# Twelve tiles' decays and the low halves move from GpSimd to VectorE, and one bit extraction from VectorE to ScalarE

## The chip, the cores and the metric

The program runs on one core of one Trainium2 chip. The metric is the device time of one execution in microseconds (us); smaller is better. TensorE (PE in the rows) multiplies matrices, VectorE (DVE), ScalarE (ACT) and GpSimd (POOL) work element by element, and SyncE (SP) issues most of the DMA transfers. Each engine takes its instructions in the order in which the program has them, and waits on semaphores for operands that another engine makes.

## The reference

Three layers follow each other over 4 sequences of 768 tokens, 512 values each, with 8 heads of 64.

```python
# retention: a decayed running state of each head
state = gamma[None, :, None, None] * state + einsum('bhd,bhe->bhde', k[:, :, t], v[:, :, t])
y[:, :, t] = scale * einsum('bhd,bhde->bhe', q[:, :, t], state)
...
# a dense layer, 512 -> 2048 -> 512, weights in float64
h = x @ w_in
g = np.maximum(h, 0.0) + alpha * np.minimum(h, 0.0)
x = g @ w_out
...
# 8 experts, 512 -> 1024 -> 512; a token goes to the one of its largest logit
logits = xn @ en.T / tau
expert_idx = np.argmax(logits, axis=1)
h = np.maximum(x[mask] @ w1[e], 0.0)
out[mask] = gate_w[mask, None] * (h @ w2[e])
```

## The kernel before

**Tiles.** The 3072 tokens are 24 tiles of 128. Tile i is chunk i // 4 of sequence i % 4, and four tiles (one chunk of each sequence) make a block of the dense layer, so there are 6 blocks. Matrix products of the dense and expert layers run in float16 with each operand cut into two halves: a high half, rounded to float16, and a low half, which is what is left. Three products (high by high, high by low, low by high) replace one in float32.

**Retention of a tile** (`att_load`, `att_hat`, `att_a`, `att_b`). Queries, keys by dimension, keys by token and values come in four parts of 128x512 float32 (`qk_buf` holds the first three, `vp_buf` the values; the first eight tiles also use the memory of `wout`, which waits for its weights). `att_hat` multiplies queries and both forms of the keys by powers of gamma: for tiles 0 to 7 two of the three products are on VectorE and one on GpSimd, from tile 8 on all three are on GpSimd. The results go to `hat_buf` or `stage`. `att_a` makes the scores and masks them on VectorE (rows `wout<-bank,cau`, `vp_buf<-bank,cau`). `att_b` makes the output and the new state `st_bd`, and cuts the output into halves `xh`, which a DMA transposes into `xT`.

**Float64 weights** (`convert`). They are loaded as integers into three buffers (`f_buf` twice, `pay_buf`), 16 pairs of chunks of 128x1024: ScalarE takes the high words as float32 and rescales them, VectorE shifts 13 bits out of the low word's upper half and masks the sign (two uint16 instructions on a 128x1024 strided view), VectorE merges the parts (`win<-win,f_buf` and the like), and ScalarE sums the squares. `quarter` and `split_out` then cut `win` and `wout` into halves with `split`: ScalarE makes the high half; the low half is VectorE's for even pairs and GpSimd's for odd ones, and for the latter ScalarE first scales the pair in float32.

**The dense layer.** `mm1(j, m)` makes step m (of 16) of block j's hidden layer, `mm2(j, m, o)` adds it to the output of tile o. `mm1` takes its PSUM bank from a ring of two (`h_ring`) and its buffer `g` from a ring of two. In block 0 ScalarE copies the bank twice (`g<-bank`, `stage<-bank`), VectorE combines them, ScalarE rounds to the high half and GpSimd subtracts for the low half. In the later blocks ScalarE makes one copy, VectorE reads the bank itself, and VectorE makes the low half too.

**The head.** I call head what runs until `mm2` keeps TensorE busy: the retention of tiles 0 to 11, all 16 conversions, the 16 hidden-layer steps of block 0, and the splits. No step of `mm2` can start before all of w_in and w_out are converted, since the scale `s_g` of w_out's halves is taken over all of them (`scale_out`); `unit_experts` (some 30 small instructions on VectorE) stands beside it.

**What sets the order.** The class `Plan` records all instructions and issues them by a list schedule: each engine takes, of what is ready by the plan's own cost table, what TensorE's sequence needs first. So a change of instructions or of engines changes the order on every engine.

Of the kernel before, what the change touches and what calls it, by code (L numbers as in the profile page):

```python
# [21 lines left out]
P = 128  # L22
NCH = S // P              # chunks of a sequence
NTILE = NT // P           # token tiles: tile i is chunk i // B of sequence i % B
BT = B                    # token tiles of a block: one chunk of each sequence
# [4 lines left out]
NPRE = 2                  # tiles of the expert that has most tokens before the last block  # L30
NMIN = NTILE - NPRE       # the other tiles of tokens sorted by expert, at least
NSLOT = NMIN + E - 1      # and at most
SL = 30
CAP = NT                  # rows of an expert's region
PW = DM + 2               # words of a routed token: hi | lo | gate | id
# [3 lines left out]
# Powers of two that bring a norm into [2^(C-190.5), 2^(C-189.5)).  # L39
# [6 lines left out]
# columns of the float32 constants  # L46
# [11 lines left out]
def _constants():  # L58
# [23 lines left out]
    # decay of a query and of a key, by chunk: [c, (h2 d), 2, pair, t]  # L82
# [13 lines left out]
class Plan:  # L96
    """Records instructions in the order in which they would be right one after the other, and
    issues them in one in which each engine always takes, of the instructions whose operands are
    there, the one that is needed first. An instruction's place in the tensor engine's own
    sequence, and what waits for it, say when it is needed."""  # L100

    # from the end of an instruction to the start of another that waits for it; a DMA's issue
    # and its transfer are apart
    AFTER = {"PE": 197.0, "ACT": 145.0, "DVE": 140.0, "POOL": 100.0, "SP": 0.0}
    DMA_DONE, DMA_RATE = 940.0, 360.0
    COLD = 1500.0, 3500.0        # the tensor engine's idle time after which it is slow, and for how long
    SLACK = 8000.0
    PATIENCE = 0.7, 2000.0
    AHEAD = 60000.0          # how long before it is needed a DMA may be issued
    BACKLOG = 2500.0         # of DMA, beyond which none is issued  # L110

    def __init__(self, nc):
        self.nc = nc
        self.nodes = []
        self.log = {}            # reads and writes of a tensor: (region, node)
        self.unit_ = None
        self.pe_time = 0.0
        self.bias = 0.0
        self.vector = self.Engine(self, nc.vector, "DVE")
        self.scalar = self.Engine(self, nc.scalar, "ACT")  # L120
        self.gpsimd = self.Engine(self, nc.gpsimd, "POOL")
        self.tensor = self.Engine(self, nc.tensor, "PE")
        self.sync = self.Engine(self, nc.sync, "SP")
# [9 lines left out]
    class Engine:  # L133
# [24 lines left out]
        def cost(self, method, kw):  # L158
            """Engine's time, time until the result is there, bytes moved."""
# [69 lines left out]
    def unit(self, eng):  # L229
        """Instructions of one engine that stay together."""  # L230
        @contextmanager
        def scope():
            assert self.unit_ is None
            node = self.Node(eng)
            node.start = self.pe_time
            self.nodes.append(node)
            self.unit_ = node
            yield
            self.unit_ = None
        return scope()  # L240
# [6 lines left out]
    def issue(self):  # L247
# [19 lines left out]
        while True:  # L267
# [16 lines left out]
            # rather wait a little for what is needed earlier  # L284
# [35 lines left out]
def retention_prelu_moe_kernel(ctx: ExitStack, tc, qkv, w_in, w_out, alpha, emb, tau, w1, w2,  # L320
# [17 lines left out]
    class Ring:  # L338
        """Buffers used in turn."""
# [22 lines left out]
    def col(name):  # L362
# [5 lines left out]
    # A matrix in float32 lies two chunks of 512 columns behind the place where its halves go,  # L368
    # so that a pair's halves never land on what is still to be split.
    win = buf("win", [KF + 2, 512])  # L370
    wout = buf("wout", [KF + 2, 512])
    stage = buf("stage", [16, 512])         # experts' weights; before, halves of g
    xT = [buf(f"xT{k}", [2, KD, BW], F16) for k in range(2)]
    st_bd = buf("st_bd", [B, KD, P])
    f64_buf = buf("f64_buf", [4, 512, 2], I32)   # float64 weights; later, halves of g
# [7 lines left out]
    # the first chunk's tiles use what else waits for w_out  # L383
    room = wout.rearrange("p c x -> p (c x)")
    first = {"qk": [room[:, 1536 * k:1536 * k + 1536].rearrange("p (a x) -> p a x", a=3) for k in range(3)] + [qk_buf],
# [3 lines left out]
             "hat": [hat_buf, stage[:, 12:15]]}  # L389
# [3 lines left out]
    x2T_ring = Ring([x2T_buf[:, k] for k in range(2)])  # L393
    pay_ring = Ring([pay_buf[:, k] for k in range(4)])
# [23 lines left out]
    def pow2(ss, s, c, hb=None):  # L418
        """Powers of two by which vectors of squared norm ss are scaled, into s."""
# [10 lines left out]
    def total(acc, n):  # L430
        """Sum of acc over partitions and columns, on every partition."""
# [9 lines left out]
    def norm(ss, n, e):  # L441
        """Newton's steps on 1/sqrt; 1e-6 on top of the norm."""
# [15 lines left out]
    def split(hi, lo, src, s, pool):  # L458
        """Halves of a pair of chunks. For the Pool engine the chunks are scaled first."""
# [13 lines left out]
    def att_load(i):  # L473
        if i % B == 0:
            SP.dma_start(out=cqk_sb, in_=cqk[i // B])
        qk_t[i] = first["qk"].next() if i < B * N_ROOM else qk_buf
# [4 lines left out]
    def att_hat(i):  # L481
        """Decayed queries and keys of tile i."""
        c = i // B
        t = qk_t.pop(i)
        hat = att[i] = first["hat"].next() if i < B * N_ROOM else hat_buf
        for a in range(2):
            (G if c > 1 else V).tensor_tensor(out=hat[:, a, :], in0=t[:, a, :],
                            in1=cqk_sb[:, a].rearrange("p k t -> p (k t)"), op=ALU.mult)
        o = _COLS["ks"][0] + H * c
        G.tensor_tensor(out=hat[:, 2, :].rearrange("p (h d) -> p h d", h=H),  # L490
                        in0=t[:, 2, :].rearrange("p (h d) -> p h d", h=H),
                        in1=cst[:, o:o + H].unsqueeze(2).to_broadcast([P, H, D]), op=ALU.mult)

    def att_a(i):
        """Masked scores of tile i."""
        hat = att[i]
        ring = x_ring if i < B + N_EARLY else m_ring
        # heads of one half of the partitions share a bank
# [14 lines left out]
    # From tile HALVED on, scores and values go into their product as halves.  # L513
# [8 lines left out]
    def att_s(i):  # L522
        """Halves of the scores and values of tile i; the state, scaled as their product is."""
# [27 lines left out]
    def att_b(i, early=False):  # L551
        """Outputs of tile i, the state after it, the halves of x."""
# [48 lines left out]
    def att_x(i, src):  # L601
        """The halves of x with the model dimension on partitions."""
# [4 lines left out]
    # The exponent is rebased by a product that moves the high word's upper eight exponent  # L607
    # bits, which takes what is too small for float32 to zero.
# [4 lines left out]
    s_in = buf("s_in", [KD])        # a scale for every quarter of w_in's columns  # L613
    i_in = buf("i_in", [KD])
    s_g = buf("s_g", [KD])          # what the halves of w_out's rows of a quarter are scaled by
# [3 lines left out]
    def convert(w, g, src):  # L619
        """Pair g of chunks to float32."""  # L620
        f = f64_ring.next()
        # w_in's chunks in the order of its columns
# [8 lines left out]
        # the low word becomes the sign and the three bits that the high word's shift makes room for  # L631
        h = f.rearrange("p n t -> p (n t)").bitcast(U16).rearrange("p (n t) -> p n t", t=4)
        V.tensor_scalar(out=h[:, :, 0], in0=h[:, :, 1], scalar1=13, scalar2=None, op0=ALU.logical_shift_right)
# [4 lines left out]
    def alpha_bound():  # L638
        # |g| <= |h| sqrt(1 + sum over partitions of their largest alpha^2)
# [7 lines left out]
    def quarter(q):  # L647
        """Halves of a quarter of w_in's columns."""
# [4 lines left out]
        for g in range(2 * q, 2 * q + 2):  # L653
            p = win16[:, 2 * g:2 * g + 2]
            split(p[:, :, 0], p[:, :, 1], raw(win, 2 * g), s_in[:, q:q + 1], g % 2 )
# [15 lines left out]
    def split_out(g):  # L671
        p = wout16[:, 2 * g:2 * g + 2]
        split(p[:, :, 0], p[:, :, 1], raw(wout, 2 * g), s_g[:, g // 2:g // 2 + 1], g % 2 )

# [62 lines left out]
    class Route:  # L737
# [7 lines left out]
        def halve(self, o, acc):  # L745
            """A routed token's row: the halves of x scaled, its gate, where it is from."""
# [24 lines left out]
        def finish(self):  # L771
# [6 lines left out]
            # 1 / scale of the row; over the norm, for the logits  # L778
# [14 lines left out]
            # the first of the largest  # L793
# [7 lines left out]
            # ranks  # L801
# [17 lines left out]
            # gates  # L819
# [39 lines left out]
    g16 = {}  # L859

    def mm1(j, m):
# [11 lines left out]
        if j == 0:  # L873
            # the Pool engine takes a part while the vector engine has most to do
            gg = g16[j, m] = gg_first.next()
            u = gg.rearrange("p a x -> p (a x)").bitcast(F32)
            A.activation(out=g, in_=h, func=AF.Relu, scale=-R_G)
            A.activation(out=u, in_=h, func=AF.Copy, scale=R_G)
            V.scalar_tensor_tensor(out=g, in0=g, scalar=oma[:, m:m + 1], in1=u, op0=ALU.mult, op1=ALU.add)
            A.activation(out=gg[:, 0, :], in_=g, func=AF.Copy)  # L880
            G.tensor_tensor(out=gg[:, 1, :], in0=g, in1=gg[:, 0, :], op=ALU.subtract)
            return
        A.activation(out=g, in_=h, func=AF.Relu, scale=-1.0)
        V.scalar_tensor_tensor(out=g, in0=g, scalar=oma[:, m:m + 1], in1=h, op0=ALU.mult, op1=ALU.add)
        gg = g16[j, m] = gg_ring.next()
# [21 lines left out]
    # slots: the two tiles known early, what there is at least, what there may be  # L907
# [41 lines left out]
    def gather(t):  # L949
# [4 lines left out]
        # with the model dimension on partitions  # L954
# [377 lines left out]
```

## Time and profile before

| what | value |
|---|---|
| median of 3 runs | 1041.25 us (1040.83 to 1045.32) |
| profiled execution, first to last instruction | 1051.0 us |
| PE busy over the span | 943.4 us (90%) |
| DVE busy | 570.0 us (54%) |
| ACT busy | 492.6 us (47%) |
| POOL busy | 304.0 us (29%) |

The profiled execution is a run of its own. Its span is 9.75 us longer than the median of the timed runs. Busy shares are means over the whole span, and the head has quite other ones than the rest, so the rows below are taken by stretch.

### The profile page before, as it was taken

The numbers are of one execution on the slowest core, as the hardware profiler recorded it, in microseconds if no ns is written. First come the engines' busy times: TensorE is split into PE (matmuls) and PEld (weight loads), VectorE is DVE, ScalarE is ACT, GpSimd is POOL, SyncE is SP. The second block draws the span as 40 slices with busy tenths as digits, with TensorE's granted clock in tenths as the row PEclk, the third lists the DMA queues.
The fourth block names the chain that finished last, engine by engine and source line by source line (L and its number), as shares of the span: only waits on it lengthen the run. The fifth ranks groups of instructions, "written<-read, shape, count | busy, mean of one in ns | idle before, by whom it ended". The sixth has DMA issues, their size and how long they took to land. (4 is left out here: it accounts for less than half of the span.)

```text
span 1051.0 us, 19041 instructions
## 1 busy us (share of the span) xinstructions
PE 943.4 (90%) x7100; PEld 561.8 (53%) x7100; DVE 570.0 (54%) x1299; ACT 492.6 (47%) x865; POOL 304.0 (29%) x316
## 2 busy tenths in 40 slices
PE   5778876999999988988999899899889999998995
PEld 5664543555554544444444444444677777775763
DVE  5999999546766775567345554645712222221231
ACT  1457666546767956787667658742101010100100
POOL 1234556312342433323312321440231212113110
PEclk9887788999999989999999999999999999999998
DMA  8986532463866956876476557569575399825670
GB/s 279 307 268 193 189 129 71 114 188 91 234 197 197 251 151 213 240 201 191 171 220 164 187 181 214 157 219 316 186 201 168 72 292 315 243 65 132 151 287 21
DMA packets 129824, 201.45 MB, mean 192 GB/s; under 512 B 89726, under 2 KB 90110, under 8 KB 124608
## 3 DMA queue, kind: packets, MB, share of 16 engines
q1 hardware_dynamic: 123168, 179.42, 58.1%
q0 software_dynamic: 6560, 20.77, 5.8%
q8 instruction: 57, 0.93, 0.4%
q14 instruction: 39, 0.32, 0.1%
HBM read 204.59 MB, written 51.14 MB: 243 GB/s over the span
## 5 line engine op out<-in xcount | busy, mean ns | idle before, releaser
L145 PE MATMUL bank<-xT,win 128*128 128x512 f16 (+1 forms) x2208 | 338.9, 310 | 14.5 <-ACT g L145 7.3
L145 PEld LDWEIGHTS <-win 128*128 128x128 f16 x2400 | 186.8, 100 | 153.8 <-issue 31.9
L145 PE MATMUL bank<-wout,f_buf 128*128 128x512 f16 x960 | 227.5, 384 | 5.6 <-DVE pay_buf L145 4.8
L145 PEld LDWEIGHTS <-f_buf 128*128 128x128 f16 x960 | 92.9, 99 | 115.6 <-issue 11.4
L145 ACT ACTIVATE stage<-stage 128x1024 f16<-128x1024 f32 x96 | 101.0, 1052 | 54.9 <-DMA wsplit<-stage 46.0
L145 POOL TENSOR_TENSOR stage<-stage 128x1024 f16<-128x1024 f32 x32 | 68.2, 2131 | 146.1 <-ACT stage L145 117.8
L145 DVE SCALAR_TENSOR_TENSOR f_buf<-g,f_buf 128x512 f16<-128x512 f32 x80 | 72.7, 909 | 53.1 <-ACT f_buf L145 52.9
L145 DVE SCALAR_TENSOR_TENSOR g<-g,oma,bank 128x512 f32<-128x512 f32 x80 | 59.4, 744 | 73.5 <-ACT g L145 73.3
L145 ACT ACTIVATE st_bd<-bank 128x512 f16<-128x512 f32 x30 | 17.9, 597 | 149.7 <-PE bank L145 129.6
L145 POOL DMA_INDIRECT out<-xT,ids x25 | 25.3, 1013 | 214.4 <-DVE xT L145 181.5
L145 ACT ACTIVATE stage<-stage,se 128x1024 f16<-128x1024 f32 (+1 forms) x64 | 71.6, 1139 | 11.2 <-DVE se L145 6.5
L145 POOL TENSOR_TENSOR hat_buf<-qk_buf,cqk_sb 128x512 f32<-128x512 f32 x32 | 46.4, 1452 | 83.4 <-DMA qk_buf<-in_qkv 44.9
L145 PEld LDWEIGHTS <-wout 128*128 128x128 f16 x1152 | 65.5, 98 | 7.8 <-issue 4.8
L145 ACT ACTIVATE g<-bank 128x512 f32<-128x512 f32 x96 | 55.9, 584 | 26.0 <-PE bank L145 25.9
L145 PE MATMUL bank<-xT,wout 128*128 128x128 f16 x1056 | 62.7, 219 | 3.5 <-issue 3.4
L145 ACT ACTIVATE f_buf<-g 128x512 f16<-128x512 f32 x80 | 49.8, 622 | 34.1 <-DVE g L145 34.1
L145 PEld LDWEIGHTS <-st_bd 128*128 128x128 f16 x408 | 39.7, 99 | 45.3 <-issue 1.6
L145 DVE SCALAR_TENSOR_TENSOR st_bd<-bank,st_bd 128x512 f16<-128x512 f32 x34 | 23.5, 690 | 65.7 <-ACT st_bd L145 58.5
L145 DVE TENSOR_SCALAR xT<-bank,f_buf,cqk_sb 128x512 f32<-128x512 f32 x22 | 17.8, 809 | 67.0 <-PE bank L145 67.0
L145 PE MATMUL bank<-win,st_bd 128*128 128x512 f16 x216 | 49.4, 386 | 0.0
L145 PE MATMUL bank<-wout,stage 128*128 128x512 f16 (+1 forms) x208 | 48.8, 388 | 0.0
L145 DVE SCALAR_TENSOR_TENSOR stage<-stage,se 128x1024 f16<-128x1024 f32 x32 | 41.1, 1283 | 12.4 <-ACT stage L145 11.0
(253 smaller groups left out, 1320.9 us busy)
## 6 DMA issues: line engine op xcount, KB each, us to landing
win<-wsplit SPq DMA_DIRECT2D x56, 1024.0 KB
wout<-wsplit SPq DMA_DIRECT2D x52, 1024.0 KB
stage<-in_w SPq DMA_DIRECT2D x64, 512.0 KB
wsplit<-stage SPq DMA_DIRECT2D x64, 512.0 KB
qk_buf<-in_qkv SPq DMA_DIRECT2D x18, 768.0 KB
f_buf<-in_w_in SPq DMA_DIRECT2D x12, 512.0 KB
vp_buf<-in_qkv SPq DMA_DIRECT2D x20, 256.0 KB
f_buf<-in_w_out SPq DMA_DIRECT2D x10, 512.0 KB
```

The costliest lines, as they stand in the source:

```text
L145: call = lambda: fn(**kw)
```

## The change

It does four things.

- For tiles 0 to 11 `att_hat` multiplies the queries and the values in place on VectorE; the keys stay as they are loaded, since the values (by token) now carry the decay that both forms of the keys had. GpSimd has nothing to do for these tiles. The buffers of queries and keys are now held until `att_b` is done, and `hat_buf` and `stage` become two more of them.
- In `convert` the shift of the low word becomes a ScalarE instruction that writes whole words.
- `split` of w_in and w_out uses VectorE for the low half of every pair, with no scaling in float32 ahead of it.
- `mm1` of block 0 does what the later blocks do: one ScalarE copy, VectorE reads the bank, VectorE makes the low half.

```diff
-             "hat": [hat_buf, stage[:, 12:15]]}
+    first = {"qk": [... for k in range(3)] + [qk_buf, hat_buf, stage[:, 12:15]],
...
+    qk_ring = Ring([qk_buf, hat_buf])
...
-        qk_t[i] = first["qk"].next() if i < B * N_ROOM else qk_buf
+        qk_t[i] = (first["qk"] if i < B * N_ROOM else qk_ring).next() if i < HALVED else qk_buf
...
-        hat = att[i] = first["hat"].next() if i < B * N_ROOM else hat_buf
+        o = _COLS["ks"][0] + H * c
+        decay = cst[:, o:o + H].unsqueeze(2).to_broadcast([P, H, D])
+        if i < HALVED:
+            att[i] = t
+            V.tensor_tensor(out=t[:, 0, :], in0=t[:, 0, :], in1=cqk_sb[:, 0].rearrange("p k t -> p (k t)"), op=ALU.mult)
+            v = v_t[i].rearrange("p (h d) -> p h d", h=H)
+            V.tensor_tensor(out=v, in0=v, in1=decay, op=ALU.mult)
+            return
+        hat = att[i] = hat_buf
         for a in range(2):
-            (G if c > 1 else V).tensor_tensor(out=hat[:, a, :], in0=t[:, a, :],
+            G.tensor_tensor(out=hat[:, a, :], in0=t[:, a, :],
...
-        V.tensor_scalar(out=h[:, :, 0], in0=h[:, :, 1], scalar1=13, scalar2=None, op0=ALU.logical_shift_right)
+        A.activation(out=f[:, :, 0], in_=h[:, :, 1], func=AF.Copy, scale=2.0 ** -13, bias=2.0 ** -14 - 0.5)
...
-            split(p[:, :, 0], p[:, :, 1], raw(win, 2 * g), s_in[:, q:q + 1], g % 2 )
+            split(p[:, :, 0], p[:, :, 1], raw(win, 2 * g), s_in[:, q:q + 1], False)
...
-        split(p[:, :, 0], p[:, :, 1], raw(wout, 2 * g), s_g[:, g // 2:g // 2 + 1], g % 2 )
+        split(p[:, :, 0], p[:, :, 1], raw(wout, 2 * g), s_g[:, g // 2:g // 2 + 1], False)
...
-        if j == 0:
-            gg = g16[j, m] = gg_first.next()
-            u = gg.rearrange("p a x -> p (a x)").bitcast(F32)
-            A.activation(out=g, in_=h, func=AF.Relu, scale=-R_G)
-            A.activation(out=u, in_=h, func=AF.Copy, scale=R_G)
-            V.scalar_tensor_tensor(out=g, in0=g, scalar=oma[:, m:m + 1], in1=u, op0=ALU.mult, op1=ALU.add)
-            A.activation(out=gg[:, 0, :], in_=g, func=AF.Copy)
-            G.tensor_tensor(out=gg[:, 1, :], in0=g, in1=gg[:, 0, :], op=ALU.subtract)
-            return
         A.activation(out=g, in_=h, func=AF.Relu, scale=-1.0)
         V.scalar_tensor_tensor(out=g, in0=g, scalar=oma[:, m:m + 1], in1=h, op0=ALU.mult, op1=ALU.add)
-        gg = g16[j, m] = gg_ring.next()
+        gg = g16[j, m] = (gg_ring if j else gg_first).next()
```

HALVED is 12 in both kernels; from that tile on nothing changes in `att_hat`.

How the instructions move shows at two places. The first is VectorE where the first hidden-layer steps come in, between the retention of tiles 4 to 7 (one piece of the difference; `g_86` and `g_87` are the two buffers `g`, `bank_93` and `bank_94` the two banks of `mm1`, the uint16 rows `f_buf<-f_buf` belong to the conversions):

```order
 L145 TENSOR_TENSOR st_bd<-bank_96,st_bd 64x4x64 x2
-L145 TENSOR_SCALAR f_buf<-f_buf 128x1024
+L145 SCALAR_TENSOR_TENSOR g_86<-g_86,oma,bank_93 128x512
+L145 TENSOR_TENSOR vp_buf<-vp_buf,cst 128x512
+L145 SCALAR_TENSOR_TENSOR g_87<-g_87,oma,bank_94 128x512
+L145 SCALAR_TENSOR_TENSOR stage<-g_86,stage 128x512
+L145 SCALAR_TENSOR_TENSOR stage<-g_87,stage 128x512
 L145 TENSOR_SCALAR hbx<-ssx_130 128x1
 L145 TENSOR_SCALAR sx_132<-hbx 128x1
-L145 TENSOR_SCALAR f_buf<-f_buf 128x1024
+L145 TENSOR_TENSOR qk_buf<-qk_buf,cqk_sb 128x512
```

Two shifts leave this place, and two hidden-layer steps, each now with two VectorE instructions, and the decays of values and queries come in.

The second place is VectorE at the end of the head, from the scale `s_g` on. Before, the first low half of w_out is followed by the experts' small instructions:

```order
L145 TENSOR_SCALAR s_g<-i_in,smn_152,so_149 128x4
L145 TENSOR_SCALAR iw<-im_151,io_150 128x1
L145 SCALAR_TENSOR_TENSOR g_86<-g_86,oma,stage 128x512
L145 TENSOR_SCALAR rd_0_188<-invx,iw 128x4
L145 TENSOR_SCALAR rd_1_189<-invx,iw 128x4
L145 SCALAR_TENSOR_TENSOR wout<-wout,s_g 128x2x512
L145 COPY ess_137<-bank_96 128x8
L145 TENSOR_SCALAR nb_0_138<-ess_137 128x8
```

In the changed kernel, same place:

```order
L145 TENSOR_SCALAR s_g<-i_in,smn_152,so_149 128x4
L145 SCALAR_TENSOR_TENSOR stage<-g_87,stage 128x512
L145 TENSOR_SCALAR sx_133<-hbx 128x1
L145 SCALAR_TENSOR_TENSOR g_86<-g_86,oma,bank_93 128x512
L145 SCALAR_TENSOR_TENSOR wout<-wout,s_g 128x2x512
L145 SCALAR_TENSOR_TENSOR xh<-bank_96,sx_133,xh 128x512
L145 SCALAR_TENSOR_TENSOR stage<-g_86,stage 128x512
L145 SCALAR_TENSOR_TENSOR wout<-wout,s_g 128x2x512
L145 SCALAR_TENSOR_TENSOR g_87<-g_87,oma,bank_94 128x512
```

The low halves of w_out, eight now on VectorE instead of four, stand closer together behind the scale, and the small instructions of the experts come between and behind them.

## Rows read from the trace of the kernel before

**Rows 1.** The page: the span, and VectorE's busy tenths in 40 equal slices.

```profile
span 1051.0 us, 19041 instructions
...
DVE  5999999546766775567345554645712222221231
```

**Rows 2.** Windows: length, busy us of PE, PEld, DVE, ACT, POOL, clock, DMA.

```profile
0.00:24.00 24.00, 13.26 (x88) 12.19 (x89) 13.50 (x27) 3.56 (x5) 4.47 (x9) 1.00 0.81 299
24.00:162.00 138.00, 107.16 (x648) 75.10 (x647) 133.59 (x175) 82.17 (x135) 59.85 (x37) 0.84 0.69 210
162.00:205.00 43.00, 34.40 (x200) 18.66 (x201) 32.88 (x75) 25.88 (x40) 21.69 (x15) 0.88 0.35 98
205.00:300.00 95.00, 93.03 (x630) 50.03 (x630) 58.55 (x155) 60.14 (x121) 26.96 (x38) 1.00 0.58 164
```

**Rows 3.** Waits of VectorE, 24 to 162 us: total us, times, longest.

```profile
DVE hbx L145 <- ACT wout L145: 1.5, 3, 0.6
DVE g L145 <- ACT g L145: 1.2, 1, 1.2
```

**Rows 4.** Waits of TensorE, 24 to 162 us, the two longest.

```profile
PE bank L145 <- DVE xh L145: 10.1, 3, 6.5
PE bank L145 <- ACT g L145: 7.3, 2, 6.6
```

**Rows 5.** VectorE's groups by shape, 24 to 162 us: count | busy us, mean ns.

```profile
L145 DVE TENSOR_SCALAR f_buf<-f_buf 128x1024 uint16<-128x1024 uint16 x21 | 33.2, 1580 | 0.1
L145 DVE TENSOR_SCALAR pay_buf<-pay_buf 128x1024 uint16<-128x1024 uint16 x10 | 16.9, 1693 | 0.0
L145 DVE SCALAR_TENSOR_TENSOR g<-g,oma,stage 128x512 f32<-128x512 f32 x14 | 15.8, 1132 | 1.2 <-ACT g L145 1.2
...
L145 DVE SCALAR_TENSOR_TENSOR win<-win,f_buf 128x1024 int32<-128x1024 int32 x6 | 8.6, 1426 | 0.0
...
L145 DVE SCALAR_TENSOR_TENSOR win<-win,s_in 128x1024 f16<-128x1024 f32 x4 | 6.8, 1704 | 0.0
...
L145 DVE TENSOR_TENSOR wout<-bank,cau 128x512 f32<-128x512 f32 x8 | 5.2, 684 | 0.1
L145 DVE TENSOR_TENSOR smn<-smn,s_in 128x1 f32<-128x1 f32 x2 | 4.2, 2088 | 0.0
...
L145 DVE SCALAR_TENSOR_TENSOR win<-win,pay_buf 128x1024 int32<-128x1024 int32 x2 | 3.5, 1752 | 0.0
```

**Rows 6.** VectorE's timeline, 103.5 to 111 us: start, us, instruction.

```profile
103.54 1.31 DVE L145 TENSOR_SCALAR f_buf<-f_buf 128x1024 uint16<-128x1024 uint16 x1
104.65 0.71 DVE L145 SCALAR_TENSOR_TENSOR g<-g,oma,stage 128x512 f32<-128x512 f32 x1
105.29 1.27 DVE L145 SCALAR_TENSOR_TENSOR win<-win,s_in 128x1024 f16<-128x1024 f32 x1
106.48 2.28 DVE L145 TENSOR_SCALAR f_buf<-f_buf 128x1024 uint16<-128x1024 uint16 x1
108.56 2.10 DVE L145 TENSOR_TENSOR smn<-smn,s_in 128x1 f32<-128x1 f32 x1
110.58 1.21 DVE L145 SCALAR_TENSOR_TENSOR wout<-wout,f_buf 128x1024 int32<-128x1024 int32 x1
```

**Rows 7.** GpSimd's timeline in the same stretch.

```profile
106.39 1.18 POOL L145 TENSOR_TENSOR stage<-g,stage 128x512 f16<-128x512 f32 x1 [7.64 <-ACT stage L145]
107.78 2.85 POOL L145 TENSOR_TENSOR win<-win 128x1024 f16<-128x1024 f32 x1 [0.21 <-ACT win L145]
```

**Rows 8.** ScalarE's groups by shape, 24 to 162 us.

```profile
L145 ACT ACTIVATE stage<-bank 128x512 f32<-128x512 f32 x14 | 8.2, 591 | 0.0
...
L145 ACT ACTIVATE win<-f_buf 128x1024 f32<-128x1024 f32 x5 | 5.7, 1135 | 0.0
```

**Rows 9.** Sum over the six stretches of 24 to 162 us at a granted clock near 0.5.

```profile
sum 44.50, PE 37.24 PEld 26.52 DVE 43.66 ACT 21.06 POOL 9.63; mean PE 6.21 PEld 4.42 DVE 7.28 ACT 3.51 POOL 1.60
```

**Rows 10.** Waits of TensorE, 162 to 205 us, the longest.

```profile
PE bank L145 <- DVE ss_b L145: 6.0, 1, 6.0
```

More of the change, by code (lines that the diff above doesn't have):

```diff
@@ L384, in retention_prelu_moe_kernel @@
     room = wout.rearrange("p c x -> p (c x)")
-    first = {"qk": [room[:, 1536 * k:1536 * k + 1536].rearrange("p (a x) -> p a x", a=3) for k in range(3)] + [qk_buf],
+    first = {"qk": [room[:, 1536 * k:1536 * k + 1536].rearrange("p (a x) -> p a x", a=3) for k in range(3)] + [qk_buf, hat_buf, stage[:, 12:15]],
              "v": [room[:, 4608 + 512 * k:5120 + 512 * k] for k in range(2)] + v_ring.bufs,
@@ L388, in retention_prelu_moe_kernel @@
              "xh": [room[:, 7680 + 512 * k:8192 + 512 * k].bitcast(F16).rearrange("p (a x) -> p a x", a=2) for k in range(3)] + xh_ring.bufs,
-             "hat": [hat_buf, stage[:, 12:15]]}
+             }
     first = {k: Ring(v) for k, v in first.items()}
@@ L484, in att_hat @@
         t = qk_t.pop(i)
-        hat = att[i] = first["hat"].next() if i < B * N_ROOM else hat_buf
+        o = _COLS["ks"][0] + H * c
[7 more added lines that the diff above has]
+        hat = att[i] = hat_buf
         for a in range(2):
-            (G if c > 1 else V).tensor_tensor(out=hat[:, a, :], in0=t[:, a, :],
+            G.tensor_tensor(out=hat[:, a, :], in0=t[:, a, :],
                             in1=cqk_sb[:, a].rearrange("p k t -> p (k t)"), op=ALU.mult)
-        o = _COLS["ks"][0] + H * c
         G.tensor_tensor(out=hat[:, 2, :].rearrange("p (h d) -> p h d", h=H),
                         in0=t[:, 2, :].rearrange("p (h d) -> p h d", h=H),
-                        in1=cst[:, o:o + H].unsqueeze(2).to_broadcast([P, H, D]), op=ALU.mult)
+                        in1=decay, op=ALU.mult)
     def att_a(i):
```

## Prediction

> **What bounds the kernel now.** I read the page first. The span is 1051.0 us, and VectorE's slices show 9 in the second to fourth slice of 26 us, then 5 to 7 [rows 1]; so there is an early stretch where it is full. The windows by stage say where. From 24 to 162 us (162 is about where the first low half of w_out becomes possible) VectorE is busy 133.59 of 138.00 us, TensorE 107.16, ScalarE 82.17, GpSimd 59.85, and the DMA share is 0.69 [rows 2]. From 205 to 300 us TensorE is busy 93.03 of 95.00 us: from there on it is the bound, and what comes earlier or later at its start is carried to the end one for one.
>
> The waits confirm the order of blame in the head. VectorE waits for others 1.5 + 1.2 us in all of the 138 us [rows 3]; TensorE waits 10.1 us for VectorE's halves of x, and 7.3 us for ScalarE's `g`, which waits for a buffer at the end of the chain VectorE, GpSimd [rows 4]. So up to 162 us VectorE sets the time, and each microsecond taken off its queue is worth one, as long as its next operands are there.
>
> **What GpSimd costs VectorE.** A uint16 instruction of a conversion takes 1.31 us and the next begins after 1.11 us, but the one at 106.48 takes 2.28 [rows 6]; a GpSimd instruction had begun at 106.39 and run to 107.57 [rows 7]. The next, on one element per partition, takes 2.10 us beside a GpSimd instruction of 2.85 [rows 6, 7]. The instructions that read PSUM don't show it: the masks have a mean of 684 ns [rows 5].
>
> How much it is, by group: busy time less count times the duration alone. uint16: 33.2 + 16.9 - 31 x 1.31 = 9.5 us. `g`: 15.8 - 14 x 0.71 = 5.9. Low halves of w_in: 6.8 - 4 x 1.27 = 1.7. The two tiny minima: 4.2 less 0.4 (I allow 0.2 each) = 3.8. The merges are four groups, of which the first and last are shown; 16 instructions, at 1.21 alone and by the two shown means 1.43 to 1.75: (8.6 + 3.5) - 8 x 1.21 = 2.4 for the shown half, so about 5 for all [rows 5, 6]. The sum is **26 us** of the 138.
>
> At this place the Trainium skill (page "SBUF — State Buffer", section "Who interferes with whom") has a rule: a VectorE instruction with two SBUF inputs, or in a two-port mode, contends with GpSimd's reads for a shared port pair and the loser waits for the whole other instruction, while one with a single SBUF input outside those modes does not contend. The trace agrees for the two-input rows and the masks; the uint16 rows have one input, and 2.28 against 1.31 us. By the rule, without a two-port mode, their 9.5 us would have another cause; about half would stay with the shifts and masks that are left, and the gain below would be 5 us smaller.
>
> **The change, part by part**, on VectorE up to the first low half of w_out, with start-to-start steps where rows give them. The shifts go: 16 x 1.11 = -17.8 us [rows 6]. The low halves of w_in's four odd pairs come: 4 x 1.19 (105.29 to 106.48) = +4.8. The hidden layer's low halves, 13 by then in the new order, have no row of their own; they have the shape of `g` but for a float16 side, 0.64 from start to start alone and 1.13 as the mean beside GpSimd [rows 5, 6]; with GpSimd quiet I take 0.64: +8.3 (14.7 at the other end). The decays: two on VectorE for each of tiles 0 to 7 as before, and 8 new ones for tiles 8 to 11; the nearest row is the mask, 0.68 with 0.07 of overlap: 8 x 0.61 = +4.9. `g` itself now reads the bank, and is taken at the same 0.64. Sum: **+0.2 us**, with 0 to +7 as ends.
>
> GpSimd is not quite silent: tile 12's three products may still fall into the stretch. Each can hold up one instruction by 2.28 - 1.31 = 1 us: I take 2 us, between 0 and 3. So VectorE's work up to the first low half falls by 26 - 0 - 2 = **24 us**: fed without gaps, it would stand after 114 us where it now stands after 138, both counted from 24 us.
>
> Will it be fed? TensorE's 107.16 us contain 37.24 at half the clock (six stretches near 0.50, that is 1.2 of 2.4 GHz) [rows 2, 9]; all at the full clock it would be 107.2 - 18.6 = 88.6, or 78% of 114; with none regained, 94%. ScalarE: 82.2 + 16 x 1.14 (the moved shift, priced by `win<-f_buf`, of the same size and stride) - 13 x 0.59 - 4 x 1.14 (scaling in float32, same shape) = 88 us, 77% [rows 2, 8]. A uint16 source on ScalarE has no row; half a microsecond more each would be +8, still under 114. DMA: 0.69 x 138 = 95 us, 83%. None is a bound by itself, but VectorE's margin over the others gets thin, and its queue is in order. I put **6 us** of new waits on it; the lower end is 0 and the upper 14, where TensorE keeps its 107 us and two thirds of its 30.8 idle ones (128 us).
>
> **The end of the head.** From 162 to 205 us TensorE idles 43.0 - 34.4 = 8.6 us, 6.0 of it for `ss_b`, tile 12's squares, queued on VectorE behind the experts' small instructions [rows 2, 10]. VectorE gets 4 x 1.19 + 3 x 0.64 = 6.7 us more there, and loses waits like the 2.10 us for one element. In the new order four low halves follow the scale closely. I take **5 us** gained, between 0 and 8.6.
>
> Before 24 us TensorE has 13.26 us of work, and the first decays wait for loads in either kernel: nothing. Beyond the head no instruction is added; the list schedule may move some, which I put at 0 within 3 us.
>
> **Sum.** 24 - 6 + 5 = 23 us less. The profiled span would be 1051.0 - 23 = 1028. The span is 9.75 us over the median, and I take that as equal in both; the median goes from 1041.25 to 1018. A change of 0.5% (5 us) is about what can be told from none here.
>
> **Rivals.**
> - *The queue is handed on.* VectorE is relieved, but then the loops of VectorE, TensorE and ScalarE set the pace, with TensorE often at the half clock: new waits of 16 us in place of 6, and 2 in place of 5 at the end: 24 - 16 + 2 = 10, so 1031. For it: TensorE at up to 94%. Against it: what TensorE waited for was mostly VectorE.
> - *The uint16 instructions stay slow.* If their 9.5 us aren't GpSimd's, the 15 or 16 that are left keep 0.3 us each: 5 us less gain, 1023. Against it: 1.31 and 2.28 us for one shape within 3 us, as GpSimd starts [rows 6, 7]. The Trainium skill's rule quoted above, read so that these instructions use one port, is this case.
> - *Everything is regained.* VectorE stays fed (0) and TensorE's gaps at the end close: 24 + 8.6 = 33, so 1008. The half clock would have to be nearly gone.
> - *Slower: the banks wait for VectorE.* Before, ScalarE alone emptied the bank of `mm1` (two copies of 591 ns [rows 8]); now it is held until VectorE comes to `g` in its queue. TensorE has two banks. If each of 14 steps waits 3 us more, that is 42 against the 23 gained elsewhere: 19 slower, 1060. It decides from 23 / 14 = 1.6 us a step. Against it: ScalarE's copy waited for VectorE and GpSimd already, through `g`'s two buffers (the 7.3 us), and in the new order `g` and its low half follow each other.
> - *Nothing:* the loads. Tiles' buffers are held longer, and if the DMA share of 0.69 and order of loads were the real pace, the stretch would stay. It would need VectorE's 1.5 + 1.2 us of waits to be wrong; I leave it in the remainder.
>
> **Chances.** As forecast (1012 to 1026): 0.50. Handed on: 0.22, about a quarter of it above 1036. uint16: 0.10. Everything: 0.09. Slower: 0.07. Remainder, within 0.5%: 0.02. So faster 0.50 + 0.16 + 0.10 + 0.09 = 0.85, same 0.06 + 0.02 = 0.08, slower 0.07. The range 1004 to 1036 leaves out the slower case, the 0.08 within 0.5%, and a little below 1004.
>
> **What would show it.** Right: uint16, merges and `smn` at their durations alone up to the first low half of w_out; the place that VectorE has reached at 162 us reached at 162 - 24 + 6 = 144; VectorE busy about 95% up to there; from it TensorE nearly without gaps. Wrong: VectorE idle by more than 15 us before it, with waits on TensorE, ScalarE or loads; TensorE waiting for `g` in every step; or uint16 rows still of two lengths.

## The result and the profile after

The changed kernel takes 1026.55 us (median of 4 runs, 1023.17 to 1027.2), the kernel before beside it 1043.28 (1040.83 to 1045.38): a ratio of 0.9833 [0.9801, 0.9865], or 16.7 us less. In a later set of runs the ratio was 0.9803 [0.9767, 0.9839]. The forecast was 23 us less: 1018, in a range of 1004 to 1036.

The profiled execution took 1025.89 us, 1.8 more than its span. The page: span and VectorE's slices, which answer to [rows 1].

```profile
span 1024.1 us, 18980 instructions
...
DVE  5779998557656865566345644655812222222231
```

Windows of the same kernel, up to the start of `s_g` at 149.5 us (164.5 before) and behind it; columns as in [rows 2].

```profile
24.00:149.50 125.50, 106.43 (x648) 76.47 (x647) 109.06 (x183) 86.97 (x133) 5.39 (x6) 0.82 0.74 230
149.50:162.00 12.50, 11.30 (x66) 5.72 (x65) 12.32 (x23) 8.07 (x12) 1.80 (x1) 1.00 0.18 73
162.00:205.00 43.00, 38.62 (x277) 23.11 (x276) 26.71 (x77) 19.29 (x39) 8.47 (x7) 0.96 0.46 135
205.00:300.00 95.00, 93.69 (x610) 49.37 (x608) 60.96 (x150) 66.09 (x128) 32.78 (x42) 1.00 0.61 183
```

GpSimd is nearly silent (5.39 us), but VectorE is no longer full: it is busy 109.06 of 125.50 us, where [rows 2] had 133.59 of 138. Its groups by shape up to the scale, against [rows 5], show what it does in that time.

```profile
L145 DVE TENSOR_SCALAR f_buf<-f_buf 128x1024 uint16<-128x1024 uint16 x11 | 14.7, 1335 | 1.5 <-ACT f_buf L145 1.3
L145 DVE SCALAR_TENSOR_TENSOR g<-g,oma,bank 128x512 f32<-128x512 f32 x14 | 10.4, 744 | 4.2 <-ACT g L145 4.0
L145 DVE SCALAR_TENSOR_TENSOR win<-win,s_in 128x1024 f16<-128x1024 f32 x8 | 10.3, 1283 | 0.1
L145 DVE SCALAR_TENSOR_TENSOR stage<-g,stage 128x512 f16<-128x512 f32 x13 | 9.0, 690 | 0.1
...
L145 DVE TENSOR_SCALAR pay_buf<-pay_buf 128x1024 uint16<-128x1024 uint16 x5 | 6.6, 1315 | 0.1
...
L145 DVE TENSOR_TENSOR vp_buf<-vp_buf,cst 128x512 f32<-128x512 f32 x7 | 4.8, 692 | 0.5 <-DMA vp_buf<-in_qkv 0.4
```

The means have come down to about the durations alone: uint16 from 1580 and 1693 ns to 1335 and 1315, `g` from 1132 to 744, the low halves of w_in from 1704 to 1283. The waits are what has grown; first VectorE's (against 1.5 and 1.2 us in [rows 3]), then TensorE's, both from 24 us to the scale.

```profile
DVE g L145 <- ACT g L145: 4.0, 4, 1.2
DVE hbx L145 <- ACT wout L145: 3.1, 2, 2.4
DVE f_buf L145 <- ACT f_buf L145: 1.3, 2, 0.8
DVE hbx L145 <- ACT xh L145: 1.3, 1, 1.3
```

```profile
PE bank L145 <- DVE g L145: 6.6, 2, 3.8
PE bank L145 <- DVE xh L145: 6.0, 3, 4.5
```

ScalarE, for which VectorE waits, waits itself for TensorE:

```profile
ACT wout L145 <- PE bank L145: 11.5, 6, 3.6
ACT g L145 <- PE bank L145: 9.6, 5, 2.6
```

So the waits now run in a ring over three queues, each in order: VectorE waits for ScalarE, ScalarE for TensorE, TensorE for VectorE. Before, one full queue set the time.

### The profile page after: what moved, and what is told of

The parts are those of the page before. It is cut to its first block, busy times and chain, and to the rows that moved or that the text cites. A ratio compares the mean times of both kernels' runs of the same rounds, so it can differ in the third digit from the quotient of the medians.

```text
span 1024.1 us, 18980 instructions
## 1 busy us (share of the span) xinstructions
PE 938.9 (92%) x7100; PEld 564.7 (55%) x7100; DVE 546.7 (53%) x1315; ACT 493.9 (48%) x857; POOL 231.3 (23%) x272
## 4 chain that ended last, share of the span: by engine, by line
PE 43%; DMA 16%; DVE 14%; ACT 12%; issue 8%; POOL 6%; SPq 0%; ACTq 0%; POOLq 0%; DVEq 0%
PE bank L145 43%; DMA wsplit<-stage 9%; ACT stage L145 6%; POOL stage L145 3%; DMA f_buf<-in_w_in 2%; DVE f_buf L145 2%; ACT f_buf L145 2%; DVE g L145 1%; POOL nt L145 1%; DVE wout L145 1%; DMA table<-pay_buf,rposi 1%; ACT pay_buf L145 1%; DVE pay_buf L145 1%; DMA x2T_buf<-pay_buf 1%; DVE vp_buf L145 1%
## 5 line engine op out<-in xcount | busy, mean ns | idle before, releaser
L145 PE MATMUL bank<-xT,win 128*128 128x512 f16 (+1 forms) x2208 | 334.8, 309 | 14.5 <-DVE g L145 6.6
L145 ACT ACTIVATE stage<-stage 128x1024 f16<-128x1024 f32 x96 | 101.0, 1052 | 54.9 <-DMA wsplit<-stage 46.7
L145 DVE SCALAR_TENSOR_TENSOR g<-g,oma,bank 128x512 f32<-128x512 f32 x96 | 71.3, 744 | 69.9 <-ACT g L145 69.6
L145 DVE SCALAR_TENSOR_TENSOR f_buf<-g,f_buf 128x512 f16<-128x512 f32 x80 | 70.2, 878 | 55.0 <-ACT f_buf L145 54.8
L145 ACT ACTIVATE st_bd<-bank 128x512 f16<-128x512 f32 x30 | 17.9, 597 | 147.1 <-PE bank L145 147.1
L145 POOL TENSOR_TENSOR hat_buf<-qk_buf,cqk_sb 128x512 f32<-128x512 f32 x24 | 34.0, 1418 | 227.2 <-DMA cqk_sb<-in_cqk 133.0
L145 POOL DMA_INDIRECT out<-xT,ids x25 | 25.3, 1013 | 206.7 <-DVE xT L145 165.6
L145 DVE TENSOR_SCALAR xT<-bank,f_buf,cqk_sb 128x512 f32<-128x512 f32 x22 | 17.8, 810 | 65.2 <-PE bank L145 65.2
```

What stands on the lines that cost most here:

```text
L145: call = lambda: fn(**kw)
```

## The account

For each kernel I added up, over VectorE's instructions from 24 us to the scale, the duration beyond that alone (1.31 us for uint16, 1.21 for a merge, 1.27 for a low half of 1024 elements, 0.70 for 512, 0.17 for tiny ones; excesses under 0.12 left out). I call that the hold-up. "Own" is busy time less hold-up, "idle" the rest of the stretch. "Scale at" is the start of `s_g`, by which the windows end. Times are us and from one profiled execution each; the ratio is of the timed runs, to the kernel before in the same set of runs.

| kernel | ratio [95%] | scale at | own | hold-up | idle | GpSimd busy |
|---|---|---|---|---|---|---|
| before | 1 | 164.5 | 107.7 | 28.2 | 4.5 | 61.1 |
| changed | 0.9833 [0.9801, 0.9865] | 149.5 | 107.7 | 1.4 | 16.4 | 5.4 |
| e1_split_pool | 0.9866 [0.9817, 0.9915] | 153.5 | 103.6 | 6.4 | 19.5 | 17.9 |
| e2_mm1_pool | 0.9809 [0.9760, 0.9857] | 149.9 | 101.0 | 8.6 | 16.2 | 26.3 |
| e3_shift_dve | 0.9928 [0.9894, 0.9963] | 165.6 | 126.3 | 1.6 | 13.7 | 7.1 |
| e4_hat_old | 0.9789 [0.9743, 0.9835] | 146.7 | 104.6 | 7.4 | 10.7 | 33.3 |
| e5_decay_pool | 0.9830 [0.9773, 0.9886] | 149.3 | 104.1 | 2.9 | 18.3 | 18.8 |
| e6_costs | 0.9780 [0.9725, 0.9835] | 145.8 | 108.5 | 1.6 | 11.7 | 7.6 |
| e7_pool_reads | 1.0016 [0.9985, 1.0047] | 164.7 | 109.9 | 21.7 | 9.1 | 62.4 |
| e8_pool_writes | 0.9914 [0.9882, 0.9946] | 157.0 | 106.2 | 7.2 | 19.6 | 28.5 |
| e9_after_again | 0.9803 [0.9767, 0.9839] | 150.4 | 107.7 | 0.8 | 17.8 | 6.3 |
| e10_costs_hat_old | 0.9817 [0.9779, 0.9854] | 150.4 | 104.3 | 9.1 | 13.0 | 33.9 |
| e11_costs_act | 0.9596 [0.9573, 0.9618] | 143.3 | 108.1 | 1.7 | 9.5 | 6.6 |
| e12_costs_act_hat_old | 0.9673 [0.9637, 0.9709] | 151.8 | 103.3 | 7.9 | 16.6 | 31.2 |

All of the 28.2 us falls on instructions that overlap one of GpSimd's. The first row and the second make the balance: hold-up 26.8 less, own work unchanged, idle 11.9 more, the scale 14.9 earlier. At the start of block 0's routing (237.4 us before, 218.7 after) it is 18.7, so the end of the head gave 3.8; at the first output row (762.0 and 743.2) it is still 18.8.

The medians of the kernel before were 1043.28, 1052.96, 1051.48 and 1049.55 us in the four sets, so I compare ratios, and points within a trace.

## Experiments

**Parts undone, one each.** Theory: GpSimd's reads of SBUF hold VectorE up, and that is most of the gain. Rival: only the length of VectorE's own queue counts.

`e1_split_pool`: the low halves of odd pairs on GpSimd again.

```diff
-            split(p[:, :, 0], p[:, :, 1], raw(win, 2 * g), s_in[:, q:q + 1], False)
+            split(p[:, :, 0], p[:, :, 1], raw(win, 2 * g), s_in[:, q:q + 1], g % 2)
...
-        split(p[:, :, 0], p[:, :, 1], raw(wout, 2 * g), s_g[:, g // 2:g // 2 + 1], False)
+        split(p[:, :, 0], p[:, :, 1], raw(wout, 2 * g), s_g[:, g // 2:g // 2 + 1], g % 2)
```

> The changed kernel with the odd pairs' low halves back on GpSimd (and ScalarE's extra scaling). Lock theory (what was gained is that GpSimd's instructions no longer hold up VectorE's): VectorE loses 8 x 1.19 = 9.5 us of work, but 8 GpSimd instructions of 2.13 us hold it up again by about 0.43 us for each of their 17 us, 7.4: near the changed kernel, 1024 to 1030, with uint16 or two-input VectorE rows near 2.2 us wherever a GpSimd split starts first. Count theory (only the number of instructions on VectorE matters): 5 to 9 us faster than the changed kernel, 1017 to 1022, rows at their durations alone.

Own work fell by 4.1, hold-up rose by 5.0, idle by 3.1. The interval overlaps the changed kernel's, but leaves out the gain of 5 to 9 us (a ratio of 0.975 to 0.979) that the rival called for.

`e2_mm1_pool`: block 0's hidden layer as before.

```diff
+        if j == 0:
+            gg = g16[j, m] = gg_first.next()
+            u = gg.rearrange("p a x -> p (a x)").bitcast(F32)
+            A.activation(out=g, in_=h, func=AF.Relu, scale=-R_G)
+            A.activation(out=u, in_=h, func=AF.Copy, scale=R_G)
...
+            G.tensor_tensor(out=gg[:, 1, :], in0=g, in1=gg[:, 0, :], op=ALU.subtract)
+            return
...
```

> The changed kernel with block 0 of the hidden layer as before (two ScalarE copies, VectorE combines, GpSimd subtracts). Lock theory: VectorE loses 16 x 0.64 = 10 us, GpSimd gets 16 instructions of 1.2 to 1.5 us, which hold VectorE up by some 9 us: 1024 to 1031. Count theory: 5 to 10 us faster than the changed kernel, 1016 to 1022. If instead the bank that waits for VectorE's queue is what new waits come from, this run is faster too, and TensorE's wait of 6.6 us for g is gone.

Own work 6.7 less, hold-up 7.2 more, idle the same: this part of the change is worth nothing that shows, and the interval doesn't separate the two theories. TensorE's 6.6 us of waiting for VectorE's `g` are gone (1.7 for ScalarE's is left), yet the scale comes no earlier, so that wait alone didn't set the head's length.

`e3_shift_dve`: the shift on VectorE again.

```diff
-        A.activation(out=f[:, :, 0], in_=h[:, :, 1], func=AF.Copy, scale=2.0 ** -13, bias=2.0 ** -14 - 0.5)
+        V.tensor_scalar(out=h[:, :, 0], in0=h[:, :, 1], scalar1=13, scalar2=None, op0=ALU.logical_shift_right)
```

> The changed kernel with the 16 shifts back on VectorE, nothing on GpSimd. Both theories: VectorE gets 16 x 1.11 = 17.8 us more and idles 16.5 us between 24 and 150 us now. If that idle time is latency that work can fill: 4 to 10 us slower than the changed kernel, 1031 to 1037. If VectorE is still the bound to the full: 15 to 18 slower, 1042 to 1045, as slow as the kernel before. uint16 rows at 1.31 us each (lock), or at a mean near 1.6 as before, if their slowness was not GpSimd's.

Own work 18.6 more, of which VectorE's idle time took up 2.7; the scale 16.1 later, the ratio 0.0095 higher, some 10 us. (The profiled execution was the slowest of seven, 1050.96 us where the median is 1046.17.) The uint16 rows have means of 1320 and 1434 ns, not 1580 and 1693 as before. Of the parts undone this alone moves the time beyond the intervals. With GpSimd still nearly silent, the kernel is 0.7% faster than before, though its scale comes 1.1 us later: that gain comes behind the scale, where block 0's routing starts at 233.2 us in place of 237.4.

`e4_hat_old`: the decays of tiles 0 to 11 as before, with their buffers. `e5_decay_pool`: in place as in the change, but by GpSimd for tiles 8 to 11, to tell the engine from the buffers. The first diff is of e4, the second of e5.

```diff
-    first = {"qk": [... for k in range(3)] + [qk_buf, hat_buf, stage[:, 12:15]],
+    first = {"qk": [... for k in range(3)] + [qk_buf],
...
+             "hat": [hat_buf, stage[:, 12:15]]}
...
-            G.tensor_tensor(out=hat[:, a, :], in0=t[:, a, :],
+            (G if c > 1 else V).tensor_tensor(out=hat[:, a, :], in0=t[:, a, :],
```

```diff
-            V.tensor_tensor(out=t[:, 0, :], in0=t[:, 0, :], in1=cqk_sb[:, 0].rearrange("p k t -> p (k t)"), op=ALU.mult)
+            e = G if c > 1 else V
+            e.tensor_tensor(out=t[:, 0, :], in0=t[:, 0, :], in1=cqk_sb[:, 0].rearrange("p k t -> p (k t)"), op=ALU.mult)
...
-            V.tensor_tensor(out=v, in0=v, in1=decay, op=ALU.mult)
+            e.tensor_tensor(out=v, in0=v, in1=decay, op=ALU.mult)
```

> The changed kernel with the decays of tiles 0 to 11 as before (20 GpSimd products of 1.0 to 1.7 us come back, 8 of VectorE's go). Lock theory: -4.9 us of VectorE's work, +0.43 x 28 = 12 us of hold-ups: 4 to 8 us slower than the changed kernel, 1030 to 1035. Count theory: 3 to 5 us faster, 1021 to 1024. If buffers held until the end of a tile cost something in the changed kernel, this run gains that back as well.

> The changed kernel with one thing back: GpSimd, not VectorE, decays the queries and values of tiles 8 to 11 (in place, in the same buffers). VectorE loses 8 instructions of 0.69 us, 5.5 us of work, and GpSimd gains 8. The version with the old decays reached the hidden-layer scale at 146.7 us against 149.5 with the change, and lost 0.9785 of the time against 0.9833; it had VectorE's idle time at 10.6 us against 16.4. If GpSimd as the engine is what helped: VectorE's idle time falls to about 12 us, GpSimd's reads bring back about 0.43 us for each us that it is busy (some 8 to 14 us, so 3 to 6), the scale comes at 147 to 149, ratio 0.978 to 0.983. If it was the buffers that are held longer (the decayed tile in the load's own buffer): idle time stays at 15 to 17 us, the hold-up of 3 to 6 us eats the work removed, the scale comes at 149 to 151, ratio 0.982 to 0.986.

By their hold-up the old decays should have cost 4 to 8 us; instead the ratio is 0.0044 lower. They brought the scale 2.8 us earlier, by less idle time (10.7 against 16.4) in spite of 6.0 more hold-up; the in-place ones by GpSimd did not (idle 18.3). That speaks for the buffers as the source of idle time. But both ratios lie within the intervals of the changed kernel, and `e10` and `e12` below, with the same old decays, had 13.0 and 16.6 of idle time; it isn't shown.

**GpSimd's load put back without its use.** `e7_pool_reads`: GpSimd subtracts the high half from itself three times in each step of block 0, into scratch; nothing waits for it.

```diff
+    scr = buf("scr", [512], F16)
...
+        if j == 0:
+            for _ in range(3):
+                G.tensor_tensor(out=scr, in0=gg[:, 0, :], in1=gg[:, 0, :], op=ALU.subtract)
```

> The changed kernel with GpSimd work that nothing waits for: in each of the first block's 16 hidden-layer steps GpSimd subtracts the 512 elements of g's high half from themselves, three times, into a scratch tile that is never read. VectorE's instructions stay what they are. If GpSimd's reads of SBUF hold VectorE up: with some 30 to 60 us of GpSimd busy before the scale, VectorE's durations there exceed those alone by 12 to 26 us (1.4 in the changed kernel), the uint16 ones among them, and the scale comes 6 to 20 us later than 149.5; ratio 0.99 to 1.00. If only the number and length of VectorE's own instructions count (the gain being what was taken from its queue): excess under 3 us, the scale at 148 to 151, ratio 0.981 to 0.987.

The ratio is 1.0016: the whole gain is gone, though no instruction was given back to VectorE. A piece of its timeline, and GpSimd's group, of this kernel:

```profile
100.59 1.30 DVE L145 TENSOR_TENSOR vp_buf<-vp_buf,cst 128x512 f32<-128x512 f32 x1
101.81 1.52 DVE L145 SCALAR_TENSOR_TENSOR stage<-g,stage 128x512 f16<-128x512 f32 x1
103.25 2.15 DVE L145 TENSOR_SCALAR pay_buf<-pay_buf 128x1024 uint16<-128x1024 uint16 x1
105.21 2.09 DVE L145 SCALAR_TENSOR_TENSOR win<-win,s_in 128x1024 f16<-128x1024 f32 x1
107.22 2.06 DVE L145 SCALAR_TENSOR_TENSOR wout<-wout,pay_buf 128x1024 int32<-128x1024 int32 x1
109.19 0.73 DVE L145 SCALAR_TENSOR_TENSOR g<-g,oma,bank 128x512 f32<-128x512 f32 x1
```

```profile
98.74 9.45 POOL L145 TENSOR_TENSOR scr<-stage 128x512 f16<-128x512 f16 x6 [9.87 <-ACT stage L145]
```

While GpSimd runs, 98.74 to 108.19, these VectorE instructions with all operands in SBUF take 0.6 to 0.85 us more than alone. The ones that read a PSUM bank are not held up: up to the scale all 14 `g<-g,oma,bank` have a mean of 738 ns, 744 in the changed kernel. So one thing that the change did, letting `g` read the bank in place of a copy in SBUF, takes it out of GpSimd's reach.

`e8_pool_writes`: in place of reads, GpSimd only writes (three fills of 608 elements a step, behind a VectorE instruction on one column).

```diff
+    scr = [buf(f"scr{k}", [608]) for k in range(2)]
...
+        if j == 0:
+            z = scr[m % 2]
+            V.tensor_scalar(out=z[:, 0:1], in0=oma[:, m:m + 1], scalar1=1.0, scalar2=None, op0=ALU.mult)
+            for _ in range(3):
+                G.memset(z, 0.0)
```

> The changed kernel with GpSimd work that only writes: in each of the first block's 16 hidden-layer steps VectorE writes one column of a scratch tile (0.06 to 0.2 us) and GpSimd fills its 608 float32 elements three times. If writes by GpSimd hold VectorE up as its reads do: excess of VectorE's durations before the scale 8 to 20 us, the scale 5 to 15 us later than 149.5, ratio 0.988 to 1.00. If it takes GpSimd's reads: excess under 4 us, the scale at 149 to 154 with the 2 to 3 us of VectorE's own 16 writes, ratio 0.982 to 0.988.

Neither: hold-up 7.2, a little under the lower figure for reads. Pieces of the timelines of VectorE and of GpSimd show on whom it falls.

```profile
66.34 0.68 DVE L145 TENSOR_TENSOR vp_buf<-vp_buf,cst 128x512 f32<-128x512 f32 x1
66.94 0.74 DVE L145 SCALAR_TENSOR_TENSOR g<-g,oma,bank 128x512 f32<-128x512 f32 x1
67.60 1.47 DVE L145 SCALAR_TENSOR_TENSOR stage<-g,stage 128x512 f16<-128x512 f32 x2
...
78.64 1.31 DVE L145 TENSOR_SCALAR f_buf<-f_buf 128x1024 uint16<-128x1024 uint16 x1
...
81.19 2.06 DVE L145 TENSOR_SCALAR invx<-hbx 128x4 int32<-128x4 int32 x1
81.26 1.99 DVE L145 TENSOR_TENSOR hat_buf<-hat_buf,cqk_sb 128x512 f32<-128x512 f32 x1
...
114.93 3.59 DVE L145 TENSOR_SCALAR f_buf<-f_buf 128x1024 uint16<-128x1024 uint16 x1 [0.85 <-ACT f_buf L145]
```

```profile
66.42 3.34 POOL L143 MEMSET scr<- 128x608 f32 x6 [20.67 <-DVE scr L145]
...
78.78 4.44 POOL L143 MEMSET scr<- 128x608 f32 x6 [2.63 <-DVE scr L145]
...
114.01 3.35 POOL L143 MEMSET scr<- 128x608 f32 x6 [30.79 <-DVE scr L145]
```

Beside six fills (from 66.42) the instructions with two SBUF inputs run as if alone (0.68; 1.47 for two in sequence). The uint16 one at 114.93, with one input, ends 1.16 us after the last of six other fills has ended at 117.36: it stood still until then. So did `invx` at 81.19, also with one input: 2.06 us, where it takes 0.16 in the changed kernel. The two-input `hat_buf` behind it in the queue ends with it, so the sum counts this wait twice: of the 7.2 us, 4.6 are the uint16 instruction and two such `invx`, 1.7 are two instructions right behind an `invx`, and 0.8 fall beside GpSimd's work for tile 12. It also goes the other way: the uint16 instruction at 78.64 began before the fills and lost nothing, and the six fills from 78.78 took 4.44 us in place of 3.34.

This agrees with the Trainium skill (page "SBUF — State Buffer", section "Who interferes with whom"): there an instruction with two SBUF inputs contends only with GpSimd instructions that read, while of one in a two-port mode and a GpSimd instruction of either kind the one that starts first blocks the other for its whole length. The uint16 instructions behave like the latter, as the prediction had left open. Only, the Trainium skill speaks there of one instruction, and the wait at 114.93 ran through several fills in a row.

**What the idle time hangs on.** Theory: the order, which the planner chose by wrong prices (uint16 at 0.6 us, measured 1.31). Rival: loops that no order avoids. No instruction is added or removed in these. `e6_costs`, and in `e11_costs_act` the second change too:

```diff
-                fast = method in ("tensor_scalar", "tensor_copy") and n > 64
-                return 65.0 + n * (0.52 if fast else 1.05), 0.0, 0
+                return 90.0 + n * 1.03, 0.0, 0
...
-                return 30.0 + 0.9 * n + (90.0 if kw.get("accum_out") is not None else 0.0), 0.0, 0
+                return 50.0 + 1.06 * n + (90.0 if kw.get("accum_out") is not None else 0.0), 0.0, 0
```

> The changed kernel, with another table of VectorE's costs in the planner that sets the order: 90 ns and 1.03 ns an element for every operation, where the uint16 shifts and copies were priced at 65 ns and 0.52 (0.6 us for 1024 elements, where the traces have 1.31). No instruction is added or removed. If the 16.4 us of VectorE's idle time before the scale come from an order that the planner got wrong by this price: idle falls to under 10 us, the scale comes at 141 to 145 and the ratio to the kernel before is 0.974 to 0.979. If they come from the loops between TensorE at its half clock, ScalarE and VectorE, whatever the order: idle 14 to 19, the scale at 147 to 152, ratio 0.981 to 0.987.

Idle 11.7, the scale at 145.8: between the two. The ratio, 0.9780, is that of the first, but its interval reaches into both. `e9_after_again` is the changed kernel, run with the next three for comparison on one chip; `e10_costs_hat_old` has the first price and e4's diff, `e12_costs_act_hat_old` both prices and e4's diff.

> The changed kernel once more, unaltered, beside the next three on their chip, so that they can be told from it. Ratio to the kernel before 0.981 to 0.986 (0.9833 so far); the scale at 148 to 151 us, VectorE idle for 15 to 18 us before it.

> The changed kernel with both edits that had less idle time: VectorE's cost in the planner as 90 ns and 1.03 ns an element, and the decays of the first twelve tiles as before the change (a tile of their own for the result, four tiles of them by GpSimd). If the two reduce different waits: VectorE idle for 6 to 9 us before the scale, hold-up 6 to 9 us, the scale at 140 to 144, ratio 0.972 to 0.977. If they reduce the same waits, which some loop over TensorE and ScalarE then limits: idle 10 to 13, the scale at 145 to 148, ratio 0.977 to 0.981.

> The changed kernel with VectorE's costs in the planner as 90 ns and 1.03 ns an element and ScalarE's as 50 and 1.06 (30 and 0.9 before; the trace has 591 ns for 512 elements and 1135 for 1024). No instruction is added or removed. If part of VectorE's 11.7 us of idle time with VectorE's prices alone came from ScalarE's being 15% low: idle 7 to 10, the scale at 142 to 144.5, ratio 0.974 to 0.9775. If what is left are loops that no order avoids: idle 10.5 to 14, the scale at 145 to 148, ratio 0.977 to 0.982.

> All three edits: both engines' prices, and the decays of the first twelve tiles as before the change. If prices and buffers act on different waits, this is the fastest: the scale at 138 to 143, ratio 0.969 to 0.976. If not, as with the decays and VectorE's prices alone, within 2 us of it.

`e11_costs_act` had 1007.96 us (1005.67 to 1008.49) where the changed kernel had 1029.78 and the one before 1049.55: the fastest version, by 21.8 us. Only 7.1 of that had come by the scale (143.3 against 150.4); the rest, which I hadn't expected, comes later. From the scale to the last block's routing, first the changed kernel in the same set (`e9`), then this one:

```profile
150.40:698.90 548.50, 509.74 (x3026) 254.75 (x3025) 330.05 (x781) 367.72 (x654) 162.09 (x197) 1.00 0.63 190
```

```profile
143.30:673.90 530.60, 510.32 (x3036) 256.08 (x3034) 334.03 (x778) 367.85 (x654) 166.76 (x197) 0.99 0.65 194
```

The stretch is 17.9 us shorter: TensorE idles 20.3 us in place of 38.8, and is busy as long. The gain is that of ScalarE's prices, which were 16% too low for 1024 elements (952 ns by the table, 1135 in the trace): `e12` differs from `e10` by them alone, and has a ratio of 0.9673 where `e10` has 0.9817; with VectorE's prices alone (`e6`) the stretch takes 549.4 us, no less than in `e9`. So an order made by these prices cost waits of TensorE far behind the head.

`e10` fell beside its forecast (0.9817, no better than the changed kernel beside it). `e12` has most of the gain of the prices, but a scale no earlier (151.8), and is 8.0 us slower than `e11`, where it had been forecast as the fastest if prices and buffers act on different waits. Versions that differ in prices and decays alone, the changed kernel included, thus had idle times from 9.5 to 17.8 us, by an order that shifts as a whole with any of them. That the order decides much of the time is shown, by `e11` against `e9` with the same instructions; which of its places costs which wait is not. The kernel before was not run with the corrected prices, so how much of the change's own gain is due to the order it happened to get isn't shown either.

## Why the prediction was right, and where it was off

- **The number.** 1026.55 lies in the range, but 0.55 above the 1012 to 1026 that stood for "as forecast", and nearer to the 1031 of "handed on" than to 1018. The range held because it was wide enough for a term that was half its size.
- **GpSimd's hold-up, 26 us, 2 of it left.** Right: 28.2 to 1.4. `e7` shows that GpSimd instructions that read cause it, and that it costs the time while VectorE's own work is nearly unchanged (109.9).
- **The uint16 rival.** Refuted: 1335 and 1315 ns with GpSimd silent, and `e8`.
- **VectorE's own work, +0.2.** Right: 107.7 in both. The table tells which terms matter: the moved shift took 18.6 off VectorE, and the low halves and decays put as much on.
- **New waits of 6 us.** This is the term that was mis-sized: idle time rose by 11.9, nearer to the 16 of "handed on", and the text's own sign of being wrong, VectorE idle by more than 15 us, came (16.4; busy 87% instead of the 95% named). The scale came 14.9 us earlier, not 18. The upper end of 14 was meant for a TensorE that keeps its 107 us, and it did: busy 106.43 us at a granted clock of 0.82, where [rows 2] has 107.16 at 0.84, and idle for 19.1. VectorE's list of waits, its four longest shown above, adds up to 14.0 us. The 11.9 is not fixed by the instructions: in the order of `e11` they leave VectorE idle for 9.5.
- **The half clock.** TensorE's clock was granted at 0.57 from 24 to 60 us in the changed kernel, near its lower level of 1.2 GHz (0.50), and VectorE was busy 29.10 of these 36 us. In `e8` it was 1.00 in that stretch, and VectorE was busy 26.61, which is less. So the half clock alone doesn't explain the idle time.
- **The end of the head, 5 us.** 3.8 came. TensorE idles 1.2 + 4.4 us from 149.5 to 205 in place of 8.6 from 162, and its wait for `ss_b` went from 6.0 [rows 10] to 1.9.
- **Slower: the banks wait for `g`.** Refuted: 6.6 us over 14 steps, 0.5 a step where 1.6 decides, and 7.3 before [rows 4].
- **Nothing, because of the loads.** Refuted: up to the scale VectorE waited 0.4 us for a load.
- **Beyond the head, 0 within 3.** Right: 18.7 us earlier at the first routing, 18.8 at the first output row.
- **From span to median.** That the span is 9.75 us over the median in both did not hold: in the changed kernel it is 2.45 under it (1024.1 and 1026.55). So the spans differ by 26.9 us and the medians by 16.7. Of the 8.1 us that the spans differ behind the first output row, 6.2 lie between the 18th and 19th output row, which the change doesn't touch: 16.7 us in before's profiled execution, 10.5 in the changed kernel's. In its second one (`e9`) it is 17.6, and in all 13 other profiles 16.0 to 17.9, so the short one is chance. Why it varies is open.

The sum becomes 26.8 - 0 - 11.9 + 3.8 = 18.7, between the 16.7 and the 19.8 (1049.55 to 1029.78) of the two measurements.

## What to carry to other kernels

Work that moves from GpSimd to VectorE saves only the hold-up that it caused, and pays its own length: here each such part came out even within intervals of some 5 us (`e1`, `e2`, `e4`, `e5`), while moving one instruction type from VectorE to ScalarE gave some 10 us, and reading PSUM directly took a whole group out of GpSimd's reach. When a full queue is relieved, part of what it gains (here 11.9 of 26.8 us) may go to waits between engines that were not visible as long as it was full; give them a price of their own. Where a planner sets the order, compare its prices with the durations in the trace first: correcting two of them gave as much again as the whole change (21.8 and 19.8 us on one chip).

## Not expected of the hardware

- A uint16 instruction with one input is held up by GpSimd's writes too: 3.59 us in place of 1.31 beside six fills. Beside six others three instructions with two SBUF inputs lost nothing (0.68; 1.47 for two).
- A VectorE instruction that reads PSUM lost nothing beside GpSimd: 738 ns in `e7`, 744 in the changed kernel.
- The time of one and the same program differs by up to 10 us between sets of runs (medians of 1043.28, 1052.96, 1051.48 and 1049.55 for the kernel before; the last three on three chips), more than half of what the change is worth. Whether the chip makes it isn't shown.
